# Attention and MLP on one core: the first batch's order rewritten, and five PSUM banks held as one tile

## The chip, the cores and the metric

The kernel runs on one core of a Trainium2 chip. Its engines, with the names of the profile: PE multiplies matrices into PSUM, with PEld loading its weights; ACT, DVE and POOL work on vectors, and ACT and DVE read PSUM; SP issues DMAs. Each engine takes its instructions in order; engines wait for each other by semaphores. The metric is the time of one execution on the device in microseconds, lower being better.

## The reference

Eight batches, twelve heads, 448 positions of 64 numbers, all float32. Queries and keys are normalised and scaled, attention is taken head by head, and the result goes through a layer norm and a two-layer MLP with a residual:

```python
q_n, k_n = rmsnorm(q, g_q), rmsnorm(k, g_k)
scores = (1 / sqrt(64)) * q_n @ k_n.T
attn = exp(scores - max); attn = attn / sum(attn)
x = (attn @ v) with the heads side by side            # [8, 448, 768]
xn = (x - mean) / sqrt(var + 1e-6) * g_ln
out = x + relu(xn @ w_ch1) @ w_ch2                    # 768 -> 3072 -> 768
```

## The kernel before

**Stages.** Heads are taken in pairs, six for each batch. For a pair, seven scores of up to 448 columns are made (matmul into a PSUM bank), ACT takes their exp from there into SBUF, and PE multiplies those with the values into two further banks (`oA`, `oB`). DVE divides and puts the result into the token tiles `x` and `xl`. The MLP of a batch takes three or four token tiles (384 or 512 columns): 24 chunks of the up-projection, each six matmuls into a bank and one relu by ACT into `hT`; then the down-projection, for each token tile and half of the 768 columns four steps of six matmuls into a bank and one add by DVE into `x`.

**Order.** The first batch's attention and MLP, together with the attention of the second batch, follow the list `ORDER`, written out by hand: each token calls one piece. S is a score, E its exp, V the product with the values, O its evacuation; a, d, h, n, j, k prepare keys (square, sum, root, scale, high half, low half), q-tokens the queries; K and Q turn keys and queries by matmuls with the identity, C and QC copy them out; T, A, N, X, XC are the layer norm; U and R an up-chunk and its relu; H, J, P the down-projection, its add and the store; L are loads, W weight loads behind a wait B; F is a run of filler matmuls. The table `ENGINE` names the engine of a piece where it isn't the usual one. Behind the list, `run_rest` emits the MLP chunks of batch b and, between them, steps of attention for batch b + 1, in proportion to the work done; the last batch has an MLP and no attention beside it. Everything but DVE behind the list runs in the order of the code.

**PSUM.** There are eight banks. Before, they are five pools' tiles: one for turned keys and queries (`tr`, at times a third score bank `psS3`), two for scores (`psS`), two for `oA` and `oB`, three for everything of the MLP (`psH` an up-chunk, `psC` a down sum, `psU` an up-chunk of the list, `psQ` turned queries). A buffer that is asked for again waits for the last reader of the tile that had it. The lines that matter are these:

```python
ps = self.ps_m.tile([128, 512], FP32, tag="mlp", name="psH")          # up, L1054
return self.ps_s.tile([128, 512], FP32, tag="psS", name="psS")        # score_bank, L449
self.psC = self.ps_m.tile([128, 512], FP32, tag="mlp", name="psC")    # down, L1087
```

L1056 is the up-projection's matmul and L1058 its relu; L1090 the down-projection's matmul and L1097 its add; L408 and L426 the scores, L440 their exp, L477 and L479 the products with the values; L693 to L697 and L704 the first batch's scores and exps; L879 the fillers; L108 and L116 copies and squares of keys and queries.

Of the kernel before, what the change touches and what calls it, by code (L numbers as in the profile page):

```python
# [27 lines left out]
ENGINE = dict(x.split(":") for x in """ j1:P C1:A QC0.0:A QC0.2:A qG2.0:V qm2.0:P qm2.4:P  # L28
R1.4:V XC2:A R2.2:V R2.4:V a4:P j4:P a6:P i6:V a7:P c7:V m7:P j8:P m8:P""".split())
ROOTS = {"h0": (("k0", 7),), "h1": (("k1", 7), ("q0.0", 4)), "h2": (("k2", 14), ("q0.2", 8)),  # L30
         "h3": (("k3", 14), ("q1.0", 12)), "hq": (("q2.0", 12),), "hr": (("q2.4", 6),)}
TWICE = ("0.0", "0.2", "1.0")
# [3 lines left out]
F12 a0 a1 d0 h0 sp1 spm qa0.0 n0 sp2 qt0.0 d1 qG0.0 j0 h1 k0 L4k G ql0.0 n1 F14 K0 Q0.0 j1 L4q a2  # L36
C0 k1 qa0.2 qa1.0 L4v qG0.2 d2 QC0.0 qG1.0 F2 K1 F9 S0.0.0 a3 S0.0.1 qt0.2 E0.0.1 h2 qt1.0 B0 W0
d3 W1 n2 ql0.2 h3 n3 z0 z2 za0 C1 j2 E0.0.0 F39 Q0.2 zb0 S0.1.0 k2 j3 QC0.2 E0.1.0 ql1.0 S0.1.1 F6
K2 F5 Q1.0 C2 K3 S0.2.0 E0.1.1 qa2.0 k3 C3 Q1.3 S0.2.1 K4 za2 E0.2.0 qt2.0 S0.3.0 C4 qa2.4 QC1.0
qt2.4 E0.2.1 F4 S0.3.1 E0.3.0 K5 S0.4.0 E0.3.1 S0.4.1 hq zb2 V0.0 E0.4.0 V0.1 z3 V0.2 za3 C5  # L40
E0.4.1 zb3 S0.5.0 L5k S0.5.1 V0.3 G2 E0.5.0 E0.5.1 S1.0.0 S1.0.1 E1.0.0 E1.0.1 V0.4 S1.1.0 E1.1.0
V0.5 S1.1.1 E1.1.1 QC1.3 O0.0 S1.2.0 S1.2.1 qG2.0 ql2.0 V1.0 O0.1 T0.0 E1.2.0 qm2.0 S1.3.0 E1.2.1
E1.3.0 qG2.4 V1.1 Q2.0 hr S1.3.1 S1.4.0 E1.3.1 Q2.2 V1.2 T0.1 A0 E1.4.0 S1.4.1 E1.4.1 QC2.0 S1.5.0
N0 ql2.4 qm2.4 V1.3 S1.5.1 V1.4 E1.5.0 S2.0.0 E1.5.1 X0 S2.0.1 QC2.2 E2.0.0 E2.0.1 V1.5 S2.0.2
Q2.4 O1.0 S2.1.0 XC0 L5v O1.1 E2.0.2 T1.0 T1.1 b4 a4 c4 E2.1.0 S2.1.1 U0.0 d4 L5q E2.1.1 S2.1.2 e4
S2.2.0 U0.1 R0.0 A1 E2.2.0 E2.1.2 S2.2.1 g4 N1 i4 S2.2.2 V2.0 j4 E2.2.1 QC2.4 S2.3.0 X1 E2.2.2 l4
XC1 m4 S2.3.1 E2.3.0 V2.1 E2.3.1 S2.3.2 E2.3.2 S2.4.0 E2.4.0 V2.2 k4 S2.4.1 Q6 S2.4.2 V2.3 E2.4.1
D6 S2.5.0 E2.4.2 R0.1 E2.5.0 O2.0 S2.5.1 V2.4 K6 B2 W2 C6 S2.5.2 v4 U1.0 E2.5.1 za4 v5 zb4 K7 b5
a5 E2.5.2 V2.5 S6.0 R1.0 S6.1 d5 C7 E6.0 U1.1 E6.1 c5 Q7 V6.0 S6.2 S6.3 O2.1 E6.2 E6.3 e5 T2.1 D7
U1.2 V6.1 S6.4 T2.0 za5 i5 A2 L6k S6.5 g5 j5 E6.5 E6.4 L6v U0.2 N2 V6.2 S6.6 S7.0 l5 L6q b6 a6 zb5  # L50
R1.2 batch1 V6.3 X2 E7.0 E6.6 R1.1 k5 V6.4 U0.3 L7k d6 XC2 B3 W3.0 W3.1 W3.2 W3.3 i6 S7.1 V6.5 L7q
v6 S7.2 V6.6 K8 U1.3 R0.2 E7.1 E7.2 S7.3 j6 R1.3 S7.4 O6 m5 k6 E7.4 c6 E7.3 C8 U2.0 e6 L7v za6
V7.0 U1.4 S7.5 R2.0 Q8 g6 V7.1 S7.6 V7.2 E7.6 V7.3 V7.4 D8 E7.5 K9 U2.1 S8.0 R0.3 l6 zb6 C9 R E8.0
R2.1 V7.5 S8.1 Q9 U1.5 E8.1 S8.2 S8.3 R1.4 E8.3 D9 U2.2 b7 a7 E8.2 S8.4 U2.3 S8.5 R2.2 m6 E8.4
R2.3 E8.5 R1.5 U0.4 K10 V7.6 O7 S8.6 C10 U2.4 R0.4 c7 E8.6 S9.0 i7 d7 E9.6 V8.0 Q10 S9.1 V8.1 V8.2
B4 W4.0 W4.1 W4.2 W4.3 E9.0 v7 S9.2 L8k E9.1 U2.5 D10 E9.2 R2.5 V8.3 V8.4 S9.3 V8.5 S9.4 E9.4 V8.6
L8v U0.5 e7 E9.3 S9.5 O8 S10.0 j7 V9.0 za7 V9.1 R0.5 V9.2 V9.3 E9.5 V9.4 E10.0 Q11 g7 zb7 H0.0.0
S10.1 E10.1 H0.0.1 S10.2 V9.5 D11 k7 l7 L8q S10.3 K11 E10.3 E10.2 H0.0.2 C11 S10.4 b8 a8 V9.6
E10.4 R2.4 H0.0.3 O9 H1.0.0 S10.5 c8 E10.5 H1.0.1 V10.0 m7 V10.1 d8 V10.2 e8 L9k v8 L9q L9v
S10.6 za8 i8 E10.6 H1.0.2 g8 E11.6 J0.0 Q12 V10.3 S11.0 V10.4 j8 k8 zb8 V10.5 D12 E11.0 S11.1  # L60
H1.0.3 T7 S11.2 K12 V10.6 H2.0.0 l8 L10k E11.1 E11.2 S11.3 E11.3 S11.4 H2.0.1 H2.0.2 J1.0 O10
V11.0 L10v L10q T9 C12 H2.0.3 V11.1 V11.2 S11.5 K13 V11.3 E11.4 E11.5 V11.4 S12.0 V11.5 V11.6
H0.1.0 O11 T11 Y.A H0.1.1 Y.N0 H0.1.2 H0.1.3 Y.N1 C13 S12.1 J0.1 E12.1 Y.N2 H1.1.0 H1.1.1 S12.2
Y.X0 Y.X1 Y.N3 Q13 H1.1.2 E12.0 Y.R E12.2 S12.3 D13 Y.X2 H1.1.3 Y.X3 x8 J1.1 J2.0 m8 y8 S12.4
H2.1.0 E12.4 E12.3 H2.1.1 H2.1.2 S12.5 H2.1.3 P2.0 P0.1 E12.5 J2.1 P1.1 P2.1 M
""".split()
DMA_UNIT = 8
IN_W2 = 4
BEHIND = {0: (4, 1), 2: (5, 2), 3: (6, 2), 4: (7, 2)}
# [51 lines left out]
class _Fast:  # L121


    def __init__(self, ctx, tc, sh, q, k, v, gs, g_ln, w1, w2, out):
# [33 lines left out]
        nc.vector.memset(self.tr[:, 64:128].bitcast(FP32), 0.0)  # L158
        self.xs, self.xls, self.st = {}, {}, {}
        self.units, self.loads, self.prs = {}, {}, {}  # L160
        self.late, self.preps, self.n_scores, self.sums = [], {}, 0, {}
        self.all_turned = False

# [74 lines left out]
    def pieces(self, u):  # L238
# [42 lines left out]
        def klo():  # L281
            nc.vector.tensor_tensor(out=c["khl"][:, :, 1], in0=self.loads[u][1],
                                    in1=c["khl"][:, :, 0], op=ALU.subtract)
# [56 lines left out]
    def keys_turned(self, khl, groups):  # L340
        nc, ps = self.nc, self.tr
# [57 lines left out]
    def score(self, p, i):  # L399
# [5 lines left out]
        if i == 0:  # L405
            self.open_powers(p)
        c["ps", i] = ps = self.score_bank(p)
# [8 lines left out]
    def left_score(self, p):  # L416
        nc = self.nc
        c = self.prs[p]
        c["ps", 6] = ps = self.score_bank(p)
# [9 lines left out]
    def power(self, p, i):  # L429
# [10 lines left out]
        self.nc.scalar.activation(out=o, in_=c.pop(("ps", i))[:, 0:S], func=AFT.Exp,  # L440
                                  scale=self.units[u][3][:, g:g + 1], bias=EXP_BIAS)
        if i == 6 and UNIT_PAIR[u] == p and u > 3:
            self.least(u)

    def score_bank(self, p):
# [15 lines left out]
    def value(self, p, i):  # L461
# [3 lines left out]
        if i == 0:  # L465
# [10 lines left out]
        for t in range(3):  # L476
            nc.tensor.matmul(oA[:, t, cs], E[:, ts(t, 128)], rhs,  # L477
                             start=(i == 0 and t == 0), stop=(i == 6 and t == 2))
        nc.tensor.matmul(oB[:, cs], E[:, 320:448], rhs, start=(i == 0), stop=(i == 6))  # L479
# [27 lines left out]
    def first_pieces(self):  # L507
# [37 lines left out]
        def start(c, part, g, tag):  # L545
# [4 lines left out]
            c["n"] = self.p_n.tile([128, 14, 2, D], FP16, tag=tag, name=tag)[:, 0:g]  # L550
# [5 lines left out]

        def key_unit(u, p0, m):
# [3 lines left out]
            def square():  # L561
                start(c, f"k{u}", g, "khl")
# [9 lines left out]
            def low():  # L572
                nc.vector.tensor_tensor(out=c["n"][:, :, 1], in0=k, in1=c["n"][:, :, 0],  # L573
                                        op=ALU.subtract)

            ops.update({f"a{u}": square, f"d{u}": lambda: total(c), f"n{u}": scale, f"j{u}": high, f"k{u}": low})
            for p in range(p0, p0 + m):
                ops[f"K{p}"] = lambda p=p: self.keys_turned(
                    c["n"], [7 * (p - p0) + i for i in range(7)])
                ops[f"C{p}"] = lambda p=p: self.moved(f"C{p}", kT[p], self.tr[:, 0:960])  # L580
# [6 lines left out]
        def query_part(ph, p0, p1):  # L587
# [10 lines left out]
            def square():  # L598
                start(c, f"q{tag}", g, "qn")
                for y, a in zip(src, at):  # L600
                    nc.scalar.activation(pair(c["sq"])[:, :, a], y, AFT.Square)
# [7 lines left out]
            def scale():  # L609
                r = c["r"].rearrange("p (w k) -> p w k", k=n)  # L610
                for y, a in zip(src, at):
                    nc.vector.tensor_tensor(
# [11 lines left out]
            def turn(a, b):  # L624
                c["ps", a] = ps = self.ps_m.tile([128, 1024], FP16, tag="mlp", name="psQ")
# [14 lines left out]
            def keep(a, b):  # L640
# [4 lines left out]
                self.moved(f"QC{ph}.{a}", o, c["ps", a][:, 0:w * (b - a)])  # L645
                for p in range(a, b):
# [25 lines left out]
        E, psS, o = {}, {}, {}  # L672
# [11 lines left out]
        def score(ph, p, k):  # L684
            if k == 0:
                E[ph, p] = room(ph, p)
            ps = psS[ph, p, k] = self.ps_s.tile([128, 512], FP32, tag="psS", name="psS")
# [12 lines left out]
        def power(ph, p, k):  # L700
            width = 192 if ph == 2 else 128
# [3 lines left out]
                                 scale=0.125, bias=EXP_BIAS)  # L705

        def bank(ph, half, t):
            if ph == 2 and half:
                return self.ps_m.tile([128, 3, 130], FP32, tag="mlp", name="oA")
# [3 lines left out]
        def value(ph, p):  # L713
            half, w = divmod(p, 3)
            width, tiles = (192, ((2, 0), (3, 64))) if ph == 2 else (128, ((ph, 0),))
            if w == 0:
                for t, _ in tiles:
                    o[half, t] = bank(ph, half, t)
            for i in range(7):
# [4 lines left out]
                for t, c0 in tiles:  # L724
                    nc.tensor.matmul(o[half, t][:, w, cs],  # L725
                                     E[ph, p][:, width * i + c0:width * i + c0 + 128], rhs,
                                     start=(w == 0 and i == 0), stop=(w == 2 and i == 6))
# [12 lines left out]

        def stat(t, half):
# [3 lines left out]
        def up(t, k):  # L745
            ps = o["up", t, k] = self.ps_m.tile([128, 512], FP32, tag="mlp", name="psU")
# [6 lines left out]
        def relu(t, k):  # L753
# [4 lines left out]
            else:  # L758
                nc.vector.tensor_scalar(out=out, in0=ps, scalar1=0.0, scalar2=None, op0=ALU.max)

# [31 lines left out]
    def spread_g(self, part):  # L792
# [25 lines left out]
    def second_pieces(self):  # L818
# [549 lines left out]
```

## Time and profile before

| | |
|---|---|
| runs | 591.69, 593.85, 594.91 us; median 593.85 |
| the profiled execution | 591.01 us, its span 589.4 us |
| first up-chunk of the list (L749) | starts at 34.92 us |
| granted TensorE clock | 1.00 |

The profile is of one execution. A row of the windows gives busy time and instruction count of each engine in a stretch. A row of the groups gives an operation's count, its busy time, the mean of one, and how long the engine had been idle before it, with what ended the idle time. A matmul's duration runs until its result is complete, so that of a row of matmuls each but the last shows only its issue slot: a busy PE is one that is issuing without a gap.

### The profile page before, as it was taken

What the parts mean: (1) busy time and instruction counts of PE and PEld (TensorE: products, weight loads), DVE (VectorE), ACT (ScalarE), POOL (GpSimd) and SP (SyncE); (2) the same over time, 40 slices, a digit from 0 to 9 for tenths busy, and PEclk for the clock granted to TensorE, in tenths of its full rate; (3) what the DMA queues carried; (4) which work ended last, traced back from release to release, by engine and by line L of the source; (5) the groups of instructions that cost most, each with busy time, mean ns of one, the idle gap of its engine ahead of it and who ended that gap; (6) DMA issues with size and microseconds to landing.
All of it is one profiled execution on the core that took longest, in us unless ns stands there. A gap on an engine that the chain in (4) does not pass through costs nothing.

```text
span 589.4 us, 12424 instructions
## 1 busy us (share of the span) xinstructions
PE 577.6 (98%) x4971; PEld 360.4 (61%) x4971; DVE 291.7 (49%) x636; ACT 353.0 (60%) x666; POOL 189.5 (32%) x258
## 2 busy tenths in 40 slices
PE   5899999999999999999999999999999999999997
PEld 5799976545666666545566666655566566654565
DVE  6999688345545456624446256815266222540011
ACT  5999773488752997178842797358844477124300
POOL 4648261065350665044350465342502000000000
PEclk9999999999999999999999999999999999999999
DMA  8999998573594987843779596844823220030011
GB/s 266 226 246 219 228 220 213 115 192 89 114 181 125 132 161 115 191 131 66 124 133 158 99 140 140 174 133 92 155 59 88 69 63 1 33 103 1 1 53 57
DMA packets 130321, 75.25 MB, mean 128 GB/s; under 512 B 96564, under 2 KB 120452, under 8 KB 130260
## 3 DMA queue, kind: packets, MB, share of 16 engines
q1 hardware_dynamic: 113712, 44.94, 37.3%
q0 software_dynamic: 16224, 29.27, 23.7%
q8 instruction: 40, 0.66, 0.5%
q10 hardware_dynamic: 324, 0.21, 0.1%
q14 instruction: 21, 0.17, 0.1%
HBM read 52.30 MB, written 11.01 MB: 107 GB/s over the span
## 4 chain that ended last, share of the span: by engine, by line
PE 95%; SPq 2%; DVE 1%; DMA 1%; ACT 0%; issue 0%
PE psC L1090 37%; PE psH L1056 33%; PE psS L408 8%; PE oA L477 5%; PE psU L749 4%; PE oB L479 2%; PE psS L426 2%; PE psS L693 1%; SPq L167 1%; SPq L175 1%; PE oA L725 1%; DMA qkv<-in_q_dram 1%; PE tr L345 1%; PE tr L362 0%; ACT E L704 0%; DVE khl L573 0%
## 5 line engine op out<-in xcount | busy, mean ns | idle before, releaser
L1090 PE MATMUL psC<-w,hT 128*128 128x384 f16 (+1 forms) x1368 | 235.6, 323 | 0.0
L1056 PE MATMUL psH<-xnT,w 128*128 128x512 f16 (+1 forms) x1008 | 217.3, 356 | 0.0
L440 ACT ACTIVATE E<-psS,rr_all 128x448 f16<-128x448 f32 x264 | 164.6, 636 | 58.3 <-PE psS L408 57.6
L1090 PEld LDWEIGHTS <-hT 128*128 128x128 f16 x1368 | 128.2, 98 | 75.9 <-issue 0.4
L1058 ACT ACTIVATE hT<-psH 128x512 f16<-128x512 f32 (+1 forms) x168 | 93.7, 558 | 112.3 <-PE psH L1056 110.8
L1056 PEld LDWEIGHTS <-w 128*128 128x128 f16 x1008 | 91.1, 98 | 77.0 <-issue 2.1
L408 PE MATMUL psS<-qU,kU 128*128 128x448 f16 x252 | 86.3, 352 | 0.0
L477 PEld LDWEIGHTS <-E 128*128 128x128 f16 x792 | 53.6, 98 | 34.4 <-issue 2.1
L1097 DVE SCALAR_TENSOR_TENSOR x<-psC,rs_all,x 128x384 f32<-128x384 f32 x48 | 29.0, 616 | 75.6 <-PE psC L1090 75.1
L274 POOL TENSOR_TENSOR qkv<-qkv,gprod 128x896 f32<-128x896 f32 x19 | 39.5, 2079 | 76.9 <-ACT khl L116 62.4
L477 PE MATMUL oA<-v,E 128*128 128x65 f16 x756 | 57.8, 193 | 0.1
L490 DVE RECIPROCAL rec_all<-oA 128x6 f32<-128x6 f32 x42 | 8.2, 195 | 88.6 <-PE oA L477 88.2
L167 POOL DMA_DIRECT2D qkv<-in_k_dram x14 | 11.1, 796 | 118.3 <-ACT E L440 53.4
L266 DVE TENSOR_REDUCE ssq<-khl 128x14 f32<-128x896 f32 x21 | 22.7, 1083 | 53.3 <-ACT khl L116 53.2
L479 PE MATMUL oB<-v,E 128*128 128x65 f16 x252 | 45.0, 193 | 0.1
L408 PEld LDWEIGHTS <-kU 128*128 128x128 f16 x252 | 24.3, 98 | 15.3
L266 DVE TENSOR_REDUCE ssq<-qn 128x14 f32<-128x896 f32 x21 | 22.8, 1084 | 21.1 <-ACT qn L116 21.1
L91 DVE SCALAR_TENSOR_TENSOR qn<-qkv,rr_all 128x256 f16<-128x256 f32 (+2 forms) x71 | 25.3, 416 | 15.1 <-ACT rr_all L270 15.1
L749 PE MATMUL psU<-xnT,w 128*128 128x128 f16 x432 | 27.0, 219 | 0.0
L749 PEld LDWEIGHTS <-w 128*128 128x128 f16 x432 | 25.2, 98 | 1.5 <-issue 0.4
L479 PEld LDWEIGHTS <-E 128*128 128x128 f16 x264 | 25.4, 96 | 0.3 <-DVE xl L497 0.2
L492 DVE TENSOR_TENSOR x<-oA,rec_all 128x384 f32<-128x384 f32 x42 | 23.4, 558 | 1.3
(161 smaller groups left out, 602.5 us busy)
## 6 DMA issues: line engine op xcount, KB each, us to landing
out_dram<-x SPq DMA_DIRECT2D x20, 384.0 KB, 2.6
qkv<-in_v_dram POOLq DMA_DIRECT2D x15, 384.0 KB, 6.6
qkv<-in_k_dram POOLq DMA_DIRECT2D x14, 384.0 KB, 4.0
qkv<-in_q_dram POOLq DMA_DIRECT2D x14, 384.0 KB, 4.9
w<-in_moe_w_ch_dram POOLq DMA_DIRECT2D x3, 1536.0 KB, 13.2
w<-in_moe_w_ch_dram POOLq DMA_DIRECT2D x8, 576.0 KB, 13.0
qkv<-in_q_dram SPq DMA_DIRECT2D x7, 384.0 KB, 8.0
qkv<-in_v_dram SPq DMA_DIRECT2D x6, 384.0 KB, 10.8
```

The costliest lines, as they stand in the source:

```text
L91: nc.vector.scalar_tensor_tensor(out=out, in0=x, scalar=8.0, in1=r.unsqueeze(2).broadcast_to([x.shape[0], g, D]), op0=ALU.mult, op1=ALU.mult)
L266: nc.vector.tensor_reduce(out=c["ssq"][:, n], in_=c["sq", n], axis=AX.X, op=ALU.add)
L274: _on(nc, f"i{u}", "P").tensor_tensor(out=self.loads[u][1], in0=self.loads[u][1], in1=sh.gprod.unsqueeze(1).broadcast_to([128, g, D]), op= ...
L408: self.nc.tensor.matmul(ps[:, 0:S], c["main"][:, ts(i, 128)], c["q"][:, ts(i // 3, S)], start=True, stop=True)
L440: self.nc.scalar.activation(out=o, in_=c.pop(("ps", i))[:, 0:S], func=AFT.Exp, scale=self.units[u][3][:, g:g + 1], bias=EXP_BIAS)
L477: nc.tensor.matmul(oA[:, t, cs], E[:, ts(t, 128)], rhs, start=(i == 0 and t == 0), stop=(i == 6 and t == 2))
L479: nc.tensor.matmul(oB[:, cs], E[:, 320:448], rhs, start=(i == 0), stop=(i == 6))
L749: nc.tensor.matmul(ps[:, ts(f, 128)], sh.w1[:, dc, ts(4 * k + f, 128)], self.xnT[:, dc, ts(t, 128)], start=(f == 0 and dc == 0), stop=(f = ...
L1056: nc.tensor.matmul(ps[:, 0:N], sh.w1[:, dc, ts(f, 128)], xnT[:, dc, 0:N], start=(dc == 0), stop=(dc == NDC - 1))
L1058: nc.scalar.activation(out=hT[:, f, 0:N], in_=ps[:, 0:N], func=AFT.Relu)
L1090: nc.tensor.matmul(self.psC[:, 0:g[1]], self.hT[:, f, ts(t, 128)], sh.w2[:, h, f, c:c + g[1]], start=(f == 0), stop=(f == NFF - 1))
L1097: self.nc.vector.scalar_tensor_tensor(out=x, in0=self.sums.pop((b, t, g[0]))[:, 0:g[1]], scalar=self.rs[:, b, t:t + 1], in1=x, op0=ALU.mul ...
```

## The change

**PSUM.** The pools for scores and for the MLP are gone. In their place stands one tile `five` of five banks, and lists in Python hand out its banks: `wide` (pairs of banks for two scores side by side), `free` (banks for single scores) and `idle` (banks for the MLP). A bank returns to its list when the piece that reads it has been emitted. The first batch's exps of two score banks become one instruction of 896 columns, twelve in place of 24. Keys are turned in two banks by turns, the second one borrowed from `oB`.

**Order.** `ORDER` is a new permutation: the pieces of the second phase, the scores, the up-chunks and the queues of loads stand elsewhere, fillers are 143 in place of 91, the three loads of the first weight W0, W1, W2 stand apart, and so do the parts of W3 and W4. I9 and I10 are new: a write by POOL of a few numbers into a tile, ahead of the loads of units 9 and 10, which holds those loads back. `ENGINE` has some 60 entries in place of 21. Sums and products carry their own bank, so that they may be emitted in any order.

```diff
-ENGINE = dict(x.split(":") for x in """ j1:P C1:A QC0.0:A QC0.2:A qG2.0:V qm2.0:P qm2.4:P
-R1.4:V XC2:A R2.2:V R2.4:V a4:P j4:P a6:P i6:V a7:P c7:V m7:P j8:P m8:P""".split())
+ENGINE = dict(x.split(":") for x in """ j1:P C1:A QC0.0:V QC0.2:A qG2.0:P qm2.0:V qm2.4:V R1.4:V XC2:A R2.2:A R2.4:V a4:P j4:P a6:P i6:P
...
-F12 a0 a1 d0 h0 sp1 spm qa0.0 n0 sp2 qt0.0 d1 qG0.0 j0 h1 k0 L4k G ql0.0 n1 F14 K0 Q0.0 j1 L4q a2
...
+a0 d0 h0 a1 L4k F12 n0 qa0.0 j0 F8 sp1 qt0.0 F14 d1 k0 F10 spm F5 h1 sp2 K0 qG0.0 a2 n1 F4 F2 j1
...
-BEHIND = {0: (4, 1), 2: (5, 2), 3: (6, 2), 4: (7, 2)}
+BEHIND = {0: (0, 2), 2: (5, 1), 3: (6, 1), 4: (7, 1)}
...
-        self.ps_s = pool("ps_s", 2, space=PSUM)
+        self.ps_f = pool("ps_f", 1, space=PSUM)
         self.ps_o = pool("ps_o", 1, space=PSUM)
-        self.ps_m = pool("ps_m", 3, space=PSUM)
...
+        self.five = self.ps_f.tile([128, 5, 512], FP32, name="five", tag="five")
+        self.n_wide, self.wide, self.idle, self.free, self.read, self.free_s = 0, [0, 2], [4], [], {}, False
...
+    def two_banks(self):
+
+        at = self.wide.pop(0)
+        self.n_wide += 1
+        if self.n_wide == 2 * NPAIR:
+            for x in self.wide:
+                self.wide_read(x)
+        return at, self.five[:, at:at + 2].rearrange("p b c -> p (b c)")
...
+    def score_psum(self):
+        at = self.free.pop(0)
+        ps = self.five[:, at]
+        self.read[id(ps)] = at, ps
+        return ps
...
+    def mlp_psum(self):
+        self.at = self.idle.pop(0)
+        return self.five[:, self.at]
...
-        if self.all_turned and self.n_scores % 3 == 2:
+        listed = f"S{p}.{i}" in ORDER or (i == 6 and p < THREE_LEFT)
+        if f"{p}.{i}" in THIRD if listed else self.n_scores % 3 == 2:
             return self.ps_tr.tile([128, 512], FP32, tag="tr", name="psS3")
-        return self.ps_s.tile([128, 512], FP32, tag="psS", name="psS")
+        return self.score_psum()
...
+            if ph < 2:
+                nc.scalar.activation(out=E[ph, p], in_=psS[ph, p][:, 0:896], func=AFT.Exp,
+                                     scale=0.125, bias=EXP_BIAS)
+                self.wide_read(psS["at", ph, p])
+                return
...
+        for u in (9, 10):
+            ops[f"I{u}"] = lambda u=u: nc.gpsimd.memset(self.load_tile(u)[1][:, 0, 0:1], 0.0)
...
-            ps = self.ps_m.tile([128, 512], FP32, tag="mlp", name="psH")
+            ps = self.mlp_psum()
...
             nc.scalar.activation(out=hT[:, f, 0:N], in_=ps[:, 0:N], func=AFT.Relu)
+            self.idle.append(self.at)
...
-            self.psC = self.ps_m.tile([128, 512], FP32, tag="mlp", name="psC")
+            self.sums[b, t, g[0]] = self.mlp_psum(), self.at
```

Two places of the order of instructions show the change. The first is on PE, at the first up-chunks behind the list (the MLP of the second batch), where two chunks enclose a score; `w_68` is the first weight, `xnT` the normalised tokens, `kU` and `qU` turned keys and queries, and the brackets name the engines (and their semaphores) that an instruction waits for. Before:

```order
L1056 LDWEIGHTS w_68
L1056 MATMUL psH<-xnT,w_68 128x384
L408 LDWEIGHTS kU_104
L408 MATMUL psS_3226<-qU_106,kU_104 128x448 [waits Activation_49]
L1056 LDWEIGHTS w_68
L1056 MATMUL psH<-xnT,w_68 128x384 [waits DVE_49]
```

And now:

```order
L1141 LDWEIGHTS w_68
L1141 MATMUL five<-xnT,w_68 128x384
L450 LDWEIGHTS kU_101
L450 MATMUL psS_3078<-qU_103,kU_101 128x448
L1141 LDWEIGHTS w_68
L1141 MATMUL five<-xnT,w_68 128x384 [waits Activation_49]
```

The order is the same. The second chunk waited for DVE, for an add that freed one of the three banks; now it waits for ACT. In the program as built, the count of that semaphore is that of the relu of the chunk ahead of it: the builder keeps the accesses of a tile in order as a whole, so that a write of one bank of `five` is put behind every earlier read of any of its banks, and a read behind every earlier write.

The second place is on ACT in the first batch, where the exps of the first two phases are (`qn`, `khl` are normalised queries and keys, `rt`, `rr_all`, `ssq` their roots and sums). Before:

```order
L704 ACTIVATE E<-psS 128x512 [waits PE_49]
L601 ACTIVATE qn<-qkv 128x2x128 [waits DVE_49,PE_49]
L601 ACTIVATE qn<-qkv 128x2x64
L704 ACTIVATE E<-psS 128x384 [waits PE_49]
L704 ACTIVATE E<-psS 128x512 [waits PE_49]
L704 ACTIVATE E<-psS 128x384 [waits PE_49]
L539 ACTIVATE rt<-ssq 128x12 [waits DVE_49]
```

And now:

```order
L769 ACTIVATE E<-five 128x896 [waits PE_49] x2
L864 COPY kT<-tr_121 128x960 [waits PE_49]
L122 ACTIVATE khl<-qkv 128x4x128
L122 ACTIVATE khl<-qkv 128x4x64 [waits DMAHW1_49,DMAHW0_49]
L864 COPY qU_104<-five 128x768 [waits PE_49]
L769 ACTIVATE E<-five 128x896 x2
L586 ACTIVATE rt<-ssq 128x12 [waits DVE_49]
```

Each pair of exps (512 and 384 columns) is one of 896, and the copies of turned keys and queries stand among them.

More of the change, by code (lines that the diff above doesn't have):

```diff
@@ L41 @@
[L41 to L46, printed above, removed]
@@ L281, in klo @@
         def klo():
-            nc.vector.tensor_tensor(out=c["khl"][:, :, 1], in0=self.loads[u][1],
+            _on(nc, f"k{u}", "V").tensor_tensor(out=c["khl"][:, :, 1], in0=self.loads[u][1],
                                     in1=c["khl"][:, :, 0], op=ALU.subtract)
@@ L464, in value @@
         E = c["EL"] if i == 6 else c["E"][:, i]
-        if i == 0:
+        c["seen"] = c.get("seen", 0) + 1
+        first, last = c["seen"] == 1, c["seen"] == 7
+        if first:
             c["oA"] = self.ps_o.tile([128, 3, 130], FP32, tag="oA", name="oA")
@@ L477, in value @@
             nc.tensor.matmul(oA[:, t, cs], E[:, ts(t, 128)], rhs,
-                             start=(i == 0 and t == 0), stop=(i == 6 and t == 2))
-        nc.tensor.matmul(oB[:, cs], E[:, 320:448], rhs, start=(i == 0), stop=(i == 6))
+                             start=(first and t == 0), stop=(last and t == 2))
+        nc.tensor.matmul(oB[:, cs], E[:, 320:448], rhs, start=first, stop=last)
     def evac_o(self, p):
@@ L543, in first_pieces, with room_of, start @@
             ops[name] = lambda name=name: root(name)
-        def start(c, part, g, tag):
+        flat = self.hT.rearrange("p f n -> p (f n)")
+        qn = {}
+        def room_of(part, g):
+            if part[0] == "k":
+                at = 5376 + 128 * KEYS_AT[part]
+                return flat[:, at:at + 128 * g].rearrange("p (g e d) -> p g e d", e=2, d=D)
+            tag, at = QUERIES_AT[part]
+            if tag not in qn:
+                qn[tag] = self.p_n.tile([128, 14, 2, D], FP16, tag=tag[:-1], name=tag[:-1])
+            return qn[tag][:, at:at + g]
+        def start(c, part, g):
             name, cols = place[part]
@@ L561, in square @@
             def square():
-                start(c, f"k{u}", g, "khl")
+                start(c, f"k{u}", g)
                 _square(nc, _on(nc, f"a{u}", "A"), c["sq"], k)
@@ L670, in first_pieces @@
                 ops[f"{piece}{z}"] = lambda z=z, e=e: values(z, e)
-        E, psS, o = {}, {}, {}
+        E, psS, o, seen = {}, {}, {}, {}
         def room(ph, p):
@@ L684, in score @@
         def score(ph, p, k):
-            if k == 0:
-                E[ph, p] = room(ph, p)
-            ps = psS[ph, p, k] = self.ps_s.tile([128, 512], FP32, tag="psS", name="psS")
+            E[ph, p] = room(ph, p)
+            if ph == 2:
+                ps = psS[ph, p, k] = self.score_psum()
+            else:
+                if (ph, p) not in psS:
+                    psS["at", ph, p], psS[ph, p] = self.two_banks()
+                ps = psS[ph, p][:, 512 * k:512 * k + 512]
             key, q, at = kT[p], qT[ph, p], 0
@@ L715, in value @@
             width, tiles = (192, ((2, 0), (3, 64))) if ph == 2 else (128, ((ph, 0),))
-            if w == 0:
+            seen[ph, half] = seen.get((ph, half), 0) + 1
+            first, last = seen[ph, half] == 1, seen[ph, half] == 3
+            if first:
                 for t, _ in tiles:
                     o[half, t] = bank(ph, half, t)
+                    o["at", half, t] = self.at
             for i in range(7):
@@ L726, in value @@
                                      E[ph, p][:, width * i + c0:width * i + c0 + 128], rhs,
-                                     start=(w == 0 and i == 0), stop=(w == 2 and i == 6))
+                                     start=(first and i == 0), stop=(last and i == 6))
         def out_of(ph, half):
@@ L739, in out_of @@
                     in1=rt.unsqueeze(3).broadcast_to([r.stop - r.start, 3, 2, D]), op=ALU.mult)
+            if ph == 2 and half:
+                self.idle += [o["at", 1, 2], o["at", 1, 3]]
         def stat(t, half):
@@ L876, in filler @@
             if "ps" not in warm:
[L877 removed]
+                warm["ps"] = self.ps_o.tile([128, 3, 130], FP32, tag="oA", name="psW")
             for _ in range(n):
```

140 lines of the change are left out of this document (87 added, 53 removed).

## Prediction

> **What bounds the kernel now.** First the head of the page and the stretches of the span, one row for each stage (columns: stretch, length, then busy time and instructions of each engine, granted TensorE clock, DMA share).
>
> ```profile
> span 589.4 us, 12424 instructions
> PE 577.6 (98%) x4971; PEld 360.4 (61%) x4971; DVE 291.7 (49%) x636; ACT 353.0 (60%) x666; POOL 189.5 (32%) x258
> ```
>
> ```profile
> 0.00:34.90 34.90, 27.33 (x405) 23.59 (x406) 29.90 (x61) 27.67 (x59) 19.56 (x31) 1.00 0.98 243
> 34.90:111.10 76.20, 76.20 (x1047) 61.56 (x1045) 62.83 (x119) 52.93 (x102) 31.69 (x38) 1.00 1.06 217
> 200.00:400.00 200.00, 200.00 (x1547) 117.57 (x1544) 100.31 (x228) 131.07 (x248) 84.31 (x117) 1.00 0.75 136
> 522.70:554.00 31.30, 31.30 (x148) 14.12 (x146) 0.76 (x2) 13.74 (x23) 0.00 (x0) 1.00 0.02 7
> 554.00:589.40 35.40, 31.29 (x217) 20.23 (x214) 5.16 (x9) 0.60 (x1) 0.00 (x0) 1.00 0.13 47
> ```
>
> The list ends where the chain that ended last shows the first run of PE's up-projection rows that is longer than a chunk:
>
> ```profile
> 111.08 6.47 PE psH L1056 x30
> ```
>
> From 34.90 us on PE is never idle; before that it lacks 34.90 − 27.33 = 7.6 us, beside DMA engines that are full (0.98). So the end is the sum of PE's issue slots, and every reader of PSUM hides behind PE. How it hides is seen where nothing but the up-projection runs, and at the change to the down-projection:
>
> ```profile
> 524.06 0.60 ACT L1058 ACTIVATE hT<-psH 128x512 f16<-128x512 f32 x1 [10.37 <-PE psH L1056]
> 525.35 0.60 ACT L1058 ACTIVATE hT<-psH 128x512 f16<-128x512 f32 x1 [0.70 <-PE psH L1056]
> ...
> 553.65 0.38 PE L1056 MATMUL psH<-xnT,w 128*128 128x512 f16 x1
> 553.87 31.42 PE L1090 MATMUL psC<-w,hT 128*128 128x384 f16 x216
> 554.07 0.60 ACT L1058 ACTIVATE hT<-psH 128x512 f16<-128x512 f32 x1 [0.70 <-PE psH L1056]
> ```
>
> A chunk of six matmuls takes 525.35 − 524.06 = 1.29 us. ACT's relu needs 0.60 of it and then idles 0.70, waiting for PE; PE meanwhile writes other buffers. The last three rows show the hand-over that will matter: the last matmul of a chunk starts at 553.65, PE issues the next one 0.22 later, the result is complete at 554.03 (0.16 after the issue slot), and the relu starts at 554.07 (0.04 more). PE does not wait for any of this, since psC is a tile of its own.
>
> A step of attention (a score, its exp, the product with the values) beside the down-projection:
>
> ```profile
> 300.70 0.35 PE L408 MATMUL psS<-qU,kU 128*128 128x448 f16 x1
> 300.70 0.32 PEld L477 LDWEIGHTS <-E 128*128 128x128 f16 x3
> 300.89 0.25 PE L477 MATMUL oA<-v,E 128*128 128x65 f16 x3
> ...
> 301.01 1.14 PE L1090 MATMUL psC<-w,hT 128*128 128x384 f16 x6
> ...
> 301.09 0.63 ACT L440 ACTIVATE E<-psS,rr_all 128x448 f16<-128x448 f32 x1 [0.65 <-PE psS L408]
> ```
>
> PE gives the score 0.19 us (300.70 to 300.89) and the four products 0.12 (to 301.01), and goes on with psC while ACT's exp runs from 301.09 for 0.63.
>
> **The change part by part. The PSUM tile.** All scores and all MLP sums now lie in one tile of five banks. The rows of the order above show what it does to the waits: before, an up-chunk waited for DVE, for a sum that had been added long before; now it waits for ACT, which is the relu of the chunk just ahead of it, in another bank. So a PE group that writes the tile behind a reader of it can't start until that reader is through, and the reader can't start until PE's last write is complete. That is a stall at each such place, and its price comes from these rows (columns: line, engine, operation, shapes, count, busy us, mean ns, idle before):
>
> ```profile
> L1058 ACT ACTIVATE hT<-psH 128x512 f16<-128x512 f32 x96 | 57.6, 600 | 70.5 <-PE psH L1056 70.1
> L1058 ACT ACTIVATE hT<-psH 128x384 f16<-128x384 f32 x72 | 36.1, 501 | 41.8 <-PE psH L1056 40.7
> L440 ACT ACTIVATE E<-psS,rr_all 128x448 f16<-128x448 f32 x264 | 164.6, 636 | 58.3 <-PE psS L408 57.6
> L704 ACT ACTIVATE E<-psS 128x512 f16<-128x512 f32 x18 | 10.7, 597 | 0.7 <-PE psS L693 0.2
> L704 ACT ACTIVATE E<-psS 128x384 f16<-128x384 f32 x18 | 8.8, 491 | 0.7 <-PE psS L697 0.5
> L1097 DVE SCALAR_TENSOR_TENSOR x<-psC,rs_all,x 128x384 f32<-128x384 f32 x48 | 29.0, 616 | 75.6 <-PE psC L1090 75.1
> ```
>
> ```profile
> 25.20 3.80 ACT L704 ACTIVATE E<-psS 128x512 f16<-128x512 f32 x7 [0.21 <-PE psS L693]
> ...
> 25.85 0.65 PE L693 MATMUL psS<-qU,kT 128*128 128x128 f16 x6 [0.18 <-ACT E L704]
> ```
>
> The last fence is the one kind of place where PE waits for ACT already: an exp starts at 25.20, takes 0.60 (mean of its row), and PE starts 0.05 after it. So a hand-over and back costs 0.16 + 0.04 + 0.05 = 0.25 us, plus the reader, less what PE has to issue into other tiles meanwhile. A relu of 512 columns: 0.25 + 0.60 = 0.85; of 384: 0.75. An exp of a score: 0.25 + 0.636, less 0.12 of products = 0.77. An add: 0.25 + 0.616 = 0.87. An exp of 896 columns, which the trace doesn't have: (597 − 491) / 128 = 0.83 ns a column makes 0.92 us.
>
> The places I count in the changed program's order, as PE groups that write the tile behind a reader of it: 442, 121 of them in the hand-written list and 321 behind it. 174 are behind one relu, mean 0.71 after what lies beside (a score in the transposes' bank, products): 124 us. 177 are behind one exp, at 0.77: 136 us. 53 are behind an add or an evacuation into x, at 0.83: 44 us. 38 are behind two or three readers, at 1.49: 57 us. The sum is **361 us**: 116 in the list, 245 behind it, some 40 for each full batch. Each third score escapes, since it goes to the transposes' bank; that is in the count.
>
> **What else ACT and DVE do.** Both work in order, so what stands ahead of a reader in their queues now stands in PE's way too.
>
> ```profile
> L108 ACT ACTIVATE khl<-qkv 128x896 f16<-128x896 f32 x19 | 18.4, 969 | 0.0
> L116 ACT ACTIVATE qn<-qkv 128x896 f32<-128x896 f32 x19 | 18.2, 956 | 0.0
> L116 ACT ACTIVATE khl<-qkv 128x896 f32<-128x896 f32 x18 | 17.0, 944 | 0.0
> ```
>
> These 56 (copies and squares of about 0.95 us) cost nothing where a chunk of 1.29 us runs beside them, and up to 0.55 where they stand between a relu and the exp of a score (0.95 less the 0.4 of the score). Summed over such places in the order that is 41 us at most and 0 at least; I take 20, about the middle, since nothing in the rows prefers an end. Adds behind other DVE work: 53 at 0 to 0.15 us (292 us of DVE in some 970 is 30%, times half an op of about 1 us): 0 to 8, I take 4.
>
> **The rest.** 52 more fillers cost 52 × 0.056 = 2.9 us if nothing hides them; most stand where PE waits for the loads (the 7.6 us above): 0 to 2.9, I take 1. The wide exps, 12 in place of 24, are in the price of their places. The pieces given to other engines, the weight issues moved apart on POOL and the two loads held back cost nothing in this forecast: the list is stretched by 116 us of PE's waits, and POOL (19.56 busy of 34.90, then 31.69 of 76.20) and the DMA queues get that much more time for the same work. Without that cover they would matter, which is the first rival below.
>
> **Sum**, against the profiled execution of 591.0 us (span 589.4; the median shown is 593.85, 0.5% higher): 591.0 + 361 + 20 + 4 + 1 = **977 us**. A difference under 0.5% (590.9 to 596.8) is what a measurement here can't tell from no change.
>
> **Rivals.** *The waits go by bank, or cost nothing.* Then PE stays full, as it does in before with a tile for each bank (PE writes psC from 553.87 while ACT reads psH from 554.07). What is left is the list's own gain: twelve pairs of exps of 0.597 + 0.491 become 0.92 each, and while the second phase runs, ACT does one exp behind the other (3.80 us for seven at 25.20), so up to 12 × 0.17 = 2.0 us come off: 591.0 − 2.0 = 589.0 us, within 0.5% and on the side of faster. It decides if fewer than about one in a hundred of the 442 places stalls. For it speaks only that the hardware has no need of the wait; against it, the rows of the order, where the wait on ACT stands on each chunk. The Trainium skill, "PSUM — Partial Sum Buffer", section "PSUM bank collisions raise a hardware error", says that two engines on different banks run clean, and advises to guard by bank; by that rule alone the time would be this rival's 589.0. The trace agrees with the page on the chip (the rows at 553.87 and 554.07); the waits of the built program are stricter than the page asks.
>
> *The clock falls as well.* At the start the same matmul runs at half speed until PE has worked for some time:
>
> ```profile
> 12.31 1.17 PE L879 MATMUL psW<-id 128*128 128x128 f16 x9
> ...
> 13.93 0.44 PE L879 MATMUL psW<-id 128*128 128x128 f16 x5
> ```
>
> The first nine come 0.107 us apart ((1.17 − 0.31) / 8, with 0.31 for the last one), the five behind 0.056. If stalls of a microsecond at each chunk took the clock back, PE's 577 us would about double: 977 + 570 = about 1550 us. For it: PE would be idle 40% of the time. Against it: single gaps are 0.7 to 2 us, and never a stretch without work. The Trainium skill, "TensorE: Matmul & The Clock Gate", section "Part 1: The HAM clock gate", puts the return to half speed behind an idle window of about 3.4 us; by it the gaps are too short and the sum stays 977. No row of before shows a return, so this stays open.
>
> **How the numbers follow.** The forecast has 0.90, the first rival 0.07, the falling clock 0.03. Low end of the forecast: none of the ACT and DVE work in the way, and one place in ten hidden by waits for loads, 591 + 0.9 × 361 = 916. High end: all of it, and each hand-over longer by 0.1 us: 591 + 361 + 41 + 8 + 3 + 44 = 1048. I give 910 to 1050, which holds about 0.8; it isn't stretched to 589, since the first rival has less than the 0.2 that may be left out. Slower 0.93 (forecast and clock); of the first rival's 0.07, 0.05 within 0.5% and 0.02 faster.
>
> **What would show it.** PE's busy share falls to about 60%, and its line for the up-projection gets idle time before it, released by ACT's relu, of some 100 us; at 1.00 of granted clock. In the last batch, 24 chunks of up-projection without steps take 24 × (1.29 + 0.85) = 51 us instead of 31. The list ends near 235 us instead of 111. The sums of the last down-projection are now 3.90 us apart, the add being hidden:
>
> ```profile
> 557.97 0.62 DVE L1097 SCALAR_TENSOR_TENSOR x<-psC,rs_all,x 128x384 f32<-128x384 f32 x1 [31.06 <-PE psC L1090]
> 561.87 0.62 DVE L1097 SCALAR_TENSOR_TENSOR x<-psC,rs_all,x 128x384 f32<-128x384 f32 x1 [3.28 <-PE psC L1090]
> ```
>
> They should come 3.90 + 0.87 = 4.8 apart. Full PE in the middle of the span would make the forecast wrong, and relus 1.29 us apart in the last batch would prove the first rival.

## The result, and the profile after

The changed kernel takes 1016.06 us (median of 4 runs, 1012.14 to 1016.14), the kernel before 593.57 us beside it (4 runs, 591.69 to 594.91): a ratio of 1.711, 95% interval 1.704 to 1.717. The forecast was 977 us with a range of 910 to 1050. The profiled execution has a span of 1014.6 us.

The head of the page of the changed kernel, with the clock that TensorE was granted in 40 slices of the span:

```profile
span 1014.6 us, 12551 instructions
PE 687.4 (68%) x5023; PEld 400.2 (39%) x5023; DVE 299.6 (30%) x635; ACT 361.2 (36%) x641; POOL 216.1 (21%) x275
...
PEclk8677879999998999999999899989999899979999
```

PE was busy 98% of its span before and is busy 68% of it now. ACT and DVE are busy for about as long as they were (353 and 292 us), over a longer span. The view of the waits says what ended PE's idle time (engine, line, waited for: us in total, times, longest):

```profile
PE five L1141 <- ACT E L483: 50.3, 79, 2.5
PE five L450 <- ACT hT L1143: 49.7, 83, 0.7
PE five L1176 <- DVE x L1182: 45.6, 29, 6.5
PE five L1176 <- ACT E L483: 43.4, 66, 1.0
PE five L1141 <- ACT hT L1143: 32.6, 66, 0.7
PE five L1141 <- ACT EL L483: 15.3, 12, 1.8
```

None of these rows existed before, when PE's waits behind a reader of scores were 0.4 us in all. Up-chunks (L1141), scores (L450) and down sums (L1176) all wait for readers of `five`: relus (L1143), exps (L483), adds (L1182). Most are short, and there are hundreds.

The chain that ended last, in the last batch's up-projection and then in its down-projection (start, length, work):

```profile
921.22 1.47 PE five L1141 x6
923.36 1.47 PE five L1141 x6
925.50 1.47 PE five L1141 x6
...
977.42 4.07 PE five L1176 x24
982.18 4.07 PE five L1176 x24
```

Chunks come 2.14 us apart, where they came 1.29 apart; down sums 4.76 apart instead of 3.90. The stretches of the span, read as before:

```profile
0.00:50.00 50.00, 34.23 (x432) 31.20 (x433) 29.82 (x51) 25.70 (x42) 30.00 (x37) 0.76 1.02 238
50.00:100.00 50.00, 32.66 (x384) 28.62 (x383) 23.55 (x39) 16.00 (x31) 14.34 (x13) 0.77 0.28 55
100.00:150.00 50.00, 34.25 (x359) 25.51 (x357) 18.49 (x29) 15.80 (x30) 18.63 (x21) 0.78 0.41 78
236.00:300.00 64.00, 42.98 (x291) 22.23 (x290) 16.74 (x38) 30.18 (x51) 18.83 (x26) 1.00 0.38 78
```

Behind the list PE is idle a third of the time, at a full clock in the stretch shown. In the first 150 us of the list the clock is at 0.76 to 0.78 besides, which the forecast's sum did not have.

### The profile page after: what moved, and what is told of

It is laid out like the page before. It is cut to its first block, busy times and chain, and to the rows that moved or that the text cites. A ratio compares the mean times of both kernels' runs of the same rounds, so it can differ in the third digit from the quotient of the medians.

```text
span 1014.6 us, 12551 instructions
## 1 busy us (share of the span) xinstructions
PE 687.4 (68%) x5023; PEld 400.2 (39%) x5023; DVE 299.6 (30%) x635; ACT 361.2 (36%) x641; POOL 216.1 (21%) x275
## 4 chain that ended last, share of the span: by engine, by line
PE 59%; ACT 26%; DVE 10%; issue 4%; POOL 0%; ACTq 0%; DVEq 0%; POOLq 0%
PE five L1176 23%; PE five L1141 22%; ACT E L483 11%; ACT hT L1143 9%; PE five L450 5%; PE five L829 3%; DVE x L1182 3%; DVE xn L1094 2%; ACT EL L483 1%; PE five L760 1%; ACT E L769 1%; DVE stat L1074 1%; PE psW L963 1%; PE five L468 1%; ACT khl L122 1%
## 5 line engine op out<-in xcount | busy, mean ns | idle before, releaser
L1176 PE MATMUL five<-w,hT 128*128 128x384 f16 (+1 forms) x1368 | 258.8, 339 | 97.5 <-DVE x L1182 45.6
L1141 PE MATMUL five<-xnT,w 128*128 128x512 f16 (+1 forms) x1008 | 222.7, 357 | 103.2 <-ACT E L483 50.3
L1176 PEld LDWEIGHTS <-hT 128*128 128x128 f16 x1368 | 136.4, 102 | 210.3 <-issue 146.6
L1143 ACT ACTIVATE hT<-five 128x512 f16<-128x512 f32 (+1 forms) x168 | 92.6, 551 | 320.7 <-PE five L1141 320.7
L483 ACT ACTIVATE E<-five,rr_all 128x448 f16<-128x448 f32 x193 | 121.4, 632 | 175.2 <-PE five L450 127.9
L1141 PEld LDWEIGHTS <-w 128*128 128x128 f16 x1008 | 97.8, 97 | 212.7 <-issue 143.1
L450 PE MATMUL five<-qU,kU 128*128 128x448 f16 x181 | 64.3, 360 | 75.8 <-ACT hT L1143 49.7
L524 PEld LDWEIGHTS <-E 128*128 128x128 f16 x792 | 54.2, 98 | 94.2 <-issue 63.5
L1182 DVE SCALAR_TENSOR_TENSOR x<-five,rs_all,x 128x384 f32<-128x384 f32 x48 | 29.5, 617 | 190.4 <-PE five L1176 178.9
L483 ACT ACTIVATE E<-psS,rr_all 128x448 f16<-128x448 f32 x71 | 44.6, 628 | 29.6 <-PE psS L450 29.6
L829 PE MATMUL five<-xnT,w 128*128 128x128 f16 x432 | 35.2, 254 | 12.5 <-ACT E L483 7.4
L450 PEld LDWEIGHTS <-kU 128*128 128x128 f16 x252 | 24.9, 99 | 21.2 <-issue 6.3
L365 POOL CAST v<-qkv 128x768 f16<-128x768 f32 x20 | 16.4, 822 | 68.9 <-PE oB L526 68.9
```

Source lines behind the costliest of these rows:

```text
L450: self.nc.tensor.matmul(ps[:, 0:S], c["main"][:, ts(i, 128)], c["q"][:, ts(i // 3, S)], start=True, stop=True)
L483: self.nc.scalar.activation(out=o, in_=ps[:, 0:S], func=AFT.Exp, scale=self.units[u][3][:, g:g + 1], bias=EXP_BIAS)
L524: nc.tensor.matmul(oA[:, t, cs], E[:, ts(t, 128)], rhs, start=(first and t == 0), stop=(last and t == 2))
L829: nc.tensor.matmul(ps[:, ts(f, 128)], sh.w1[:, dc, ts(4 * k + f, 128)], self.xnT[:, dc, ts(t, 128)], start=(f == 0 and dc == 0), stop=(f = ...
L1141: nc.tensor.matmul(ps[:, 0:N], sh.w1[:, dc, ts(f, 128)], xnT[:, dc, 0:N], start=(dc == 0), stop=(dc == NDC - 1))
L1143: nc.scalar.activation(out=hT[:, f, 0:N], in_=ps[:, 0:N], func=AFT.Relu)
```

## The experiments

**One tile or five.** The changed kernel with five tiles of one bank; the exps over two banks become two instructions again, since their banks are now two tiles.

```diff
-        self.five = self.ps_f.tile([128, 5, 512], FP32, name="five", tag="five")
+        self.five = [self.ps_f.tile([128, 512], FP32, name=f"b{i}", tag=f"b{i}") for i in range(5)]
...
-                nc.scalar.activation(out=E[ph, p], in_=psS[ph, p][:, 0:896], func=AFT.Exp,
-                                     scale=0.125, bias=EXP_BIAS)
+                for a, n in ((0, 512), (512, 384)):
+                    nc.scalar.activation(out=E[ph, p][:, a:a + n], in_=psS[ph, p][a // 512][:, 0:n], func=AFT.Exp,
+                                         scale=0.125, bias=EXP_BIAS)
```

> The changed kernel with five tiles of one bank each in place of one tile of five; order, engines, fillers and loads as changed; the twelve exps of two banks are two instructions again. Theory A (the waits of the one tile make the time): the stalls go, PE is full again from 35 us on at a granted clock of 1.00, 591 us within 6. Rival B (the new order and the moved engines make it): over 900 us, as before with PE idle behind ACT.

Measured: 607.93 us (5 runs), ratio to before 1.030, interval 1.027 to 1.032. The head of its page:

```profile
span 602.3 us, 12541 instructions
PE 582.7 (97%) x5023; PEld 365.9 (61%) x5023; DVE 297.4 (49%) x635; ACT 345.1 (57%) x653; POOL 216.2 (36%) x275
```

With order, engines, fillers and loads as changed, 408 of 422 us are gone and PE is at 97% again. Theory A holds for the bulk. But 607.9 is 11 us above the upper end of what it expected: something else in the change costs 3%.

**Two tiles of two banks and one of one bank**, with the wide exps kept.

```diff
-        self.five = self.ps_f.tile([128, 5, 512], FP32, name="five", tag="five")
+        self.duo = [self.ps_f.tile([128, n, 512], FP32, name=f"duo{i}", tag=f"duo{i}") for i, n in enumerate((2, 2, 1))]
...
-        return self.five[:, self.at]
+        return self.duo[self.at // 2][:, self.at % 2]
```

> The changed kernel with the five banks as three tiles of two, two and one bank, the exps of two banks kept. Theory A: only a write behind a reader of the other bank of the same pair waits; counted by the same prices some 35 us for single readers and up to 73 more where several readers lie between, so 620 to 700 us. Rival B: about 1000 us.

Measured: 694.69 us (2 runs), ratio 1.174. Only the neighbours of a pair wait for each other, and the loss falls to a quarter. Its waits show the up-chunks behind a relu 41 times, where the one tile had 66 behind a relu and 79 behind an exp:

```profile
PE duo L1176 <- DVE x L1182: 27.0, 16, 5.8
PE duo L1141 <- ACT hT L1143: 19.2, 41, 1.1
PE duo L450 <- ACT E L483: 12.1, 21, 1.2
```

**The one tile without the rest of the change.** The kernel of before, with its two score banks and three MLP banks as slices of one tile, each buffer in the bank it had.

```diff
-        self.ps_s = pool("ps_s", 2, space=PSUM)
+        self.ps_f = pool("ps_f", 1, space=PSUM)
+        one = self.ps_f.tile([128, 5, 512], FP32, name="one", tag="one")
+        self.ps_s = _Ring(one, [int(x) - 1 for x in SEQ_S])
...
-        self.ps_m = pool("ps_m", 3, space=PSUM)
+        self.ps_m = _Ring(one, [int(x) - 3 for x in SEQ_M])
```

> The kernel of before, its order and engines untouched, with the two score banks and the three MLP banks as slices of one tile, each buffer in the bank that it had. Theory A: 441 places stall, 362 us by the same prices, and with ACT's other work and a lower clock as in the changed kernel 950 to 1060 us. Rival B: 594 us as before.

Measured: 1015.27 us (2 runs), ratio 1.716, interval 1.711 to 1.720, within 1 us of the changed kernel. The page and the waits read the same:

```profile
PE 678.1 (67%) x4971; PEld 392.7 (39%) x4971; DVE 293.1 (29%) x636; ACT 369.4 (37%) x666; POOL 191.0 (19%) x258
```

```profile
PE one L430 <- ACT hT L1080: 49.7, 83, 0.7
PE one L1078 <- ACT E L462: 47.6, 78, 0.9
PE one L1112 <- DVE x L1119: 45.1, 28, 6.5
```

`_Ring` hands out the slices, in the order in which the pools had handed out their banks. So the tile alone is enough for the whole loss, and nothing else of the change is needed for it.

**Only the MLP's three banks in one tile.**

```diff
-        self.ps_m = pool("ps_m", 3, space=PSUM)
+        self.ps_f = pool("ps_f", 1, space=PSUM)
+        self.ps_m = _Ring(self.ps_f.tile([128, 3, 512], FP32, name="one", tag="one"), [int(x) - 5 for x in SEQ_M])
```

> The kernel of before with only the three MLP banks as one tile, the scores in tiles of their own. Theory A: an exp no longer stands in PE's way, 236 places with relus and adds remain, 136 us by the same prices: 700 to 790 us, and a clock nearer to 1.00. Rival B: 594 us.

Measured: 783.06 us (2 runs), ratio 1.323, near the upper end. Exps are out of PE's way; relus and adds are not:

```profile
PE one L1111 <- DVE x L1118: 59.7, 41, 6.5
PE one L1077 <- ACT hT L1079: 56.5, 128, 0.8
```

The 128 waits behind a relu are 0.44 us each, the 41 behind an add 1.46 us each. The adds are the dearer part, by their longest ones.

**What else costs 3%: the table of engines?** Five tiles, new order, `ENGINE` as before.

> Five tiles of one bank as in the first experiment, new order, but the table of engines as before. Theory C (what is left of the loss, some 15 us, is the moves of pieces between DVE and POOL, which run slow beside each other): 590 to 596 us, no DVE copy or difference above 1.1 us, PE idle before 40 us shorter by about 7 us. Rival D (the order of the pieces makes it): 603 us or more.

Measured: 612.75 us (6 runs), ratio 1.034, interval 1.031 to 1.036: not better, but 5 us worse. Theory C falls as stated. Its trace did show slow DVE work. DVE and then POOL, from two answers of the timeline:

```profile
15.39 4.99 DVE L625 TENSOR_TENSOR hT<-hT,rr_all 128x896 f32<-128x896 f32 x1
...
23.57 1.08 DVE L625 TENSOR_TENSOR hT<-hT,rr_all 128x896 f32<-128x896 f32 x1
```

```profile
15.83 1.83 POOL L664 TENSOR_TENSOR qkv<-qkv,gprod 128x768 f32<-128x768 f32 x1
17.59 0.30 POOL L727 CAST vl<-qkv 64x128 f16<-64x128 f32 x1
17.83 1.60 POOL L722 CAST v<-qkv 128x768 f16<-128x768 f32 x2
```

The same operation on DVE takes 1.08 us at 23.57 and 4.99 at 15.39, where a run of POOL operations lies beside it. In the first experiment a copy, which the kernel of before had done on POOL, took long in the same way:

```profile
32.03 3.77 DVE L679 COPY khl<-khl 128x768 f16<-128x768 f16 x1
```

**POOL kept away from DVE.** Nine casts from POOL to ACT and one product (qG1.0) from POOL to DVE, once with the engines of before and once with the new ones; in the second the doubling of the third phase's queries goes back to POOL too.

```diff
-                nc.gpsimd.tensor_copy(
+                _copy(nc, nc.scalar, self.v16[:, p0:p1, :, :, 0:D].rearrange("p s h j d -> p s (h j) d"),
...
...
-ENGINE = dict(x.split(":") for x in """ j1:P ...
+ENGINE = dict(x.split(":") for x in """ qG1.0:V j1:P ...
```

> As the experiment with the engines of before (five tiles, new order), and nine casts of the first batch's values go from POOL to ACT and one product with the gains (qG1.0) from POOL to DVE, so that POOL does nothing beside DVE from 16 to 21 us. Theory P (a DVE operation that meets a run of POOL operations waits for them: 4.99 us in place of 1.09 at 15.4 us): that operation takes about 1.1 us again, PE's wait of 6.17 us at 23.7 us shrinks to 3 us or less, 604 to 609 us against 612.75. Rival D (the order alone makes the wait): no change within 2 us.

> As the five tiles of the first experiment (new order, new engines), with the same casts on ACT and qG1.0 on DVE, and the doubling of the third phase's queries (qm2.0, qm2.4) back on POOL. Theory P: the two DVE operations of 3.87 and 3.77 us are gone, PE's waits of 3.2 and 3.55 us before 40 us shrink to 1.5 us or less together, 598 to 603 us against 607.9. Rival D: no change within 2 us.

Measured: 612.73 us (4 runs, ratio 1.034, interval 1.030 to 1.037) and 604.01 us (4 runs, ratio 1.021, interval 1.017 to 1.024). In the first the operation itself did what theory P said, 1.08 us in place of 4.99, and PE's wait went from 6.17 to 3.37 us. From the timelines of the first, DVE and PE:

```profile
15.10 1.08 DVE L625 TENSOR_TENSOR hT<-hT,rr_all 128x896 f32<-128x896 f32 x1
```

```profile
20.62 0.23 PE L383 MATMUL tr<-id,hT 128*128 128x128 f16 x1 [3.37 <-DVE hT L632]
23.87 0.85 PE L694 MATMUL b<-id,qn 128*64 128x128 f16 x12 [1.85 <-ACT v L112]
```

But a wait for ACT, which now has the casts, took its place, and the time did not move: theory P's 604 to 609 us were missed, and for the time rival D was right. In the second 4 us were gained, 1 us short of the least that was expected; a wait of 3.46 us for the same keys remains at 20.38, where 1.5 us or less was expected for two waits together. So DVE and POOL do slow each other, and taking these POOL operations away gains 4 us net of the 16; what the slowing alone costs is not shown, since ACT got the casts. What in the order makes the rest stays open: by the stretches of the first experiment PE has 29.42 us busy up to 40 us where it had 32.43, and 36.07 between 120 and 160 us where it had 40.00. By an estimate from the starts of the matmuls, the 13 us between the two profiled executions are some 7 us more of waiting, 3 to 4 of half speed (the granted clock is 0.87 up to 40 us, where it was 1.00) and 2.9 of the 52 fillers.

**The clock.** The falling clock was a rival with 0.03, and the trace shows a part of it. Two runs of the kernel of before, in which ACT reads the sums of the last batch's 24 up-chunks again ahead of the relu (the results are unused), in three levels of eight chunks. In the first all chunks share one buffer; in the second two chunks are followed by one gap of twice the length. From the first run's edit:

```diff
+                    for n in [(96,), (512,), (512, 512)][f // 8]:
+                        nc.scalar.activation(out=self.scr[:, 0:n], in_=ps[:, 0:n], func=AFT.Relu)
```

> The kernel of before; in the last batch's 24 up-chunks all sums go to one buffer and ACT reads it once or twice more ahead of the relu (results unused): chunk, gap, chunk, gap, with gaps of about 1.1, 1.45 and 2.05 us for eight chunks each (1.29 us of issue: shares 0.54, 0.47, 0.39). At full clock 24 chunks take 68 us, 628 us in all. Theory S (the clock falls with the share of work over some microseconds): half speed from the second or third level on. Theory G (it falls with the length of one gap): as the gaps say, to be compared with the next run. Rival W (only an idle window of 3.4 us brings it down): full clock throughout.

> The same with two buffers: two chunks, one gap twice as long (about 2.2, 2.9 and 4.1 us), so the same shares 0.54, 0.47 and 0.39; 628 us at full clock. Theory S: it falls at the same level as in the run before. Theory G: it falls at a level earlier. Rival W: it falls in the third level at most.

Measured: 624.2 and 638.4 us (one run each), clock 1.00 and 0.975. In the first run chunks take 1.47 us at all three levels. The chain there, at the third:

```profile
566.30 1.47 PE psH L1062 x6
...
569.62 1.47 PE psH L1062 x6
```

In the second, pairs at the end of the first level and the beginning of the second, with PE's idle time before each:

```profile
544.32 2.75 PE L1062 MATMUL psH<-xnT,w 128*128 128x512 f16 x12 [1.94 <-ACT hT L1072]
549.70 4.44 PE L1062 MATMUL psH<-xnT,w 128*128 128x512 f16 x12 [2.63 <-ACT hT L1072]
556.77 4.43 PE L1062 MATMUL psH<-xnT,w 128*128 128x512 f16 x12 [2.63 <-ACT hT L1072]
```

Idle for 1.94 us, a pair takes 2.75 us; idle for 2.63, it takes 4.44, a part of it at half speed. Yet that level's share of work was laid out at 0.47, and the first run's third level, with 1.29 of 3.32 us or 0.39, stays at full clock. So theory S falls as it was laid out, and rival W falls too, since 2.63 us were enough. Theory G fits these two runs, but not the list of the changed kernel, where half speed follows on idle times of about 1 us:

```profile
30.63 0.27 PE L760 MATMUL five<-qU,kU 128*128 128x128 f16 x2 [1.00 <-ACT E L769]
...
32.48 0.59 PE L760 MATMUL five<-qU,kT 128*128 128x128 f16 x6 [0.76 <-ACT E L769]
...
33.52 0.85 PE L760 MATMUL five<-qU,kT 128*128 128x128 f16 x6
```

The six matmuls at 33.52 take 0.85 us: less 0.31 for the last, five intervals of 0.11, which is half speed. What fits all three runs is the work in windows of a fixed length. In every trace of this case the granted clock, once it has first risen, changes only at whole steps of 3.41 us (the end of the program apart). The second run, cut at such steps:

```profile
546.55:549.97 3.42, 0.79 (x5) 0.27 (x4) 0.00 (x0) 2.42 (x5) 0.00 (x0) 1.00 0.00 0
549.97:553.38 3.41, 3.41 (x10) 1.18 (x9) 0.00 (x0) 0.00 (x0) 0.00 (x0) 0.50 0.00 0
553.38:556.79 3.41, 0.78 (x5) 0.25 (x4) 0.00 (x0) 2.42 (x5) 0.00 (x0) 1.00 0.01 2
556.79:560.21 3.42, 3.42 (x9) 1.22 (x9) 0.00 (x0) 0.00 (x0) 0.00 (x0) 0.50 0.00 0
```

Each window at 0.50 follows one in which PE was busy for 0.79 or 0.78 us. Counted in this way by the issue slots of the matmuls over all eleven traces, each of 59 falls follows a window with at most 0.40 of work, and each of the 2067 windows behind which the clock stayed full had at least 0.38, the first run's third level among them. Half speed ended behind windows with 0.72 or more and stayed behind those with 0.70 or less; one with 0.76 is the exception. So the bound for a fall is near 0.4 of 3.41 us in these traces. The length of a single gap does not decide; how little work is left in one window does.

## Why the prediction was right

**The mechanism** was right: a tile of five banks is ordered as a whole, and PE waits at each change from a reader to a write. The one tile alone gave 1015 us, five tiles gave it back.

**The prices** were right where one reader is alone. A relu was to cost 0.85 us, so that chunks would come 2.14 us apart: they do. An add was to cost 0.87: down sums come 4.76 apart, 0.86 over 3.90. By the starts of the matmuls, all intervals less their issue slots, waits behind relus come to 123 us (forecast 124), and those behind exps to 184, where the forecast had 136 for one exp alone, 57 for several readers and 20 for ACT's other work, 213 together; some 20 us of the readers' waits are behind other copies.

**The adds** were mis-sized: 44 us for themselves and 4 for other DVE work ahead of them, 75 measured. The step took DVE's other work as spread evenly. It isn't: at the end of each batch the layer norm of the next one stands in a row ahead of an add. DVE and PE there, at the last such place:

```profile
899.53 2.80 DVE L1094 SCALAR_TENSOR_TENSOR xn<-x,stat,gln 128x768 f16<-128x768 f32 x3
...
902.26 1.01 DVE L1094 SCALAR_TENSOR_TENSOR xn<-xl,stat,gln 128x768 f16<-128x768 f32 x1
903.30 0.62 DVE L1182 SCALAR_TENSOR_TENSOR x<-five,rs_all,x 128x384 f32<-128x384 f32 x1
...
903.97 7.00 PE L1176 MATMUL five<-w,hT 128*128 128x384 f16 x24 [6.53 <-DVE x L1182]
```

PE is idle 6.53 us for an add of 0.62. There are six such places, of 4.59 to 6.53 us.

**The clock** was missing from the sum. The last row shows it: these 24 matmuls take 7.00 us and the same 24 at 977.42 take 4.07. Each of the six long waits costs some 2 to 3 us more in this way, and the list runs at 0.77 for 150 us. Half speed costs 40 us in all by the matmuls' starts, against 6 before. The forecast's sign "at 1.00 of granted clock" did not come: the mean is 0.941. The rival had named the thing with the wrong size: not the whole of PE's work falls to half speed, but some 40 of its 577 us, 7%. The chance of 0.03 was for all or nothing; a term of 0 to 50 us within the forecast would have been right.

**The sum**, then: waits 403 us less the 14 of before, 389 against 385 in the forecast; half speed 35 against 0; fillers 2.9 against 1. (With the trace's record of the clock in place of the matmuls' starts the waits are 382 and half speed 40.) Over-sized exps and under-sized adds nearly cancelled, and the clock is what moved 977 to 1016.

The count of places was right in total and wrong in its parts. By the starts of the matmuls PE waits 443 times before a write of the tile (442 were counted), but 72 of these lie in the list and 371 behind it, where the forecast had 121 and 321. So its sign "the list ends near 235 us" was missed by 29 us: the first up-chunk behind the list starts at 206.02, and the two parts read so:

```profile
0.00:206.02 206.02, 138.17 (x1499) 109.16 (x1500) 100.18 (x181) 74.28 (x135) 76.87 (x85) 0.83 0.55 117
206.02:1014.60 808.58, 549.19 (x3524) 291.05 (x3523) 199.45 (x454) 286.94 (x507) 139.28 (x190) 0.97 0.26 63
```

The sum does not hang on where that line is drawn: 50 places at the mean price of 361 / 442 = 0.82 us move 41 us from the list to the rest.

**The first rival** gave 589.0 us if the waits went by bank. With a tile for each bank it is 607.9 (there the twelve exps are two each again, by the rival's own price 2.0 us). So its price was wrong and so was its sign: the new order is 2.7 to 3.2% slower than the old one even without the waits, by the interval. The rival counted the shorter exps and left the moved pieces, the fillers and the held-back loads at nothing, although their cover, the 116 us of waits that the forecast put into the list, is gone in its case; the forecast had said that they would matter then, but gave no price.

## What to carry to other kernels

Buffers that different engines use at once need tiles of their own, even where their banks are apart on the chip: look in the built order at whom the first write of each group waits for, and price it as drain, hand-over, reader and hand-over, times the number of groups. A reader that becomes part of the chain brings all that stands ahead of it in its engine's queue, which comes in runs and not evenly. When PE is made to wait, add the clock: in these traces it costs again where less than some 0.4 of 3.41 us is work.

## What the hardware showed that was not expected

The clock went to half without any long idle time. In the changed kernel from 40 to 50 us PE was busy 6.83 of 10.00 us, at a granted clock of 0.50:

```profile
40.00:50.00 10.00, 6.83 (x72) 6.28 (x70) 3.10 (x5) 3.36 (x6) 1.61 (x1) 0.50 1.12 222
```

It had fallen at 32.75 us, behind a window with 0.38 of work, and stayed at half for seven windows of 3.41 us, until one had 0.78.

The Trainium skill, "TensorE: Matmul & The Clock Gate", section "Part 1: The HAM clock gate", puts the fall behind an idle window of about 3.4 us. These runs differ from it: 2.63 us idle were enough each time, and in the list gaps of about 1 us. The length agrees: every stretch at half speed between two at full speed lasts 3.41 us or a multiple of it. But the window needn't be idle: up to 0.40 of it was work.

A DVE operation of two inputs that met a run of POOL operations took 4.99 us in place of 1.08. The Trainium skill, "SBUF — State Buffer", section "SBUF: two separate sides", has the pair of ports that the two engines share as an exclusive lock, on which the loser blocks. The trace agrees that one is kept out, and shows more: the operation is recorded from 15.39 us on, ahead of POOL's product at 15.83, and ended only at 20.38, when at least four of POOL's operations were through, not one.
